# A fused Nystrom attention and expert layer on one core: overlapping landmark transposes and another hand-written order of 1147 operations

## Chip, core and metric

The kernel runs on one core of one Trainium2 chip. The metric is the device time of one execution in microseconds (us). Five engines work in parallel, each through its own instructions in order: PE (matmul, with weight loads shown as PEld), DVE, ACT, POOL (GpSimd) and SP, which here only issues DMAs. POOL issues DMAs too.

## What is computed

Attention over 8 batches of 8 heads, 576 rows and 64 columns, with 32 landmarks per head, and behind it a mixture of 8 experts over the 4608 tokens that come out. Cut to what matters:

```
q_lm = q.reshape(B, H, 32, 18, D).mean(axis=3)        # landmarks: means of 18 rows
k_lm = k.reshape(B, H, 32, 18, D).mean(axis=3)
A, Bm, C = softmax(q k_lm^T), softmax(q_lm k_lm^T), softmax(q_lm k^T)    # each scaled
Z = Bm^T / (norms); six times Z = 2 Z - Z Bm Z
attn = A Z C v
x = attn as (tokens, 512)
e = argmax(x w_gate); gate = max(softmax(x w_gate)); eom = sigmoid(x w_output_gate)
out = gate * eom * (relu(x w1[e]) w2[e])               # per token, by its expert
```

## The kernel before

The work is a list of 1147 operations, built batch by batch in program order, each with a kind, the engines that may do it, and what it reads and writes. `Plan.op` records them; `Plan.emit` then emits them in the order of the string `ORDER`, whose words are an operation's number and a letter for the engine that does it (p PE, v DVE, a ACT, g POOL, s SP). An operation's tile is taken from its tag's free list when its first operation is emitted, and given back behind its last. So `ORDER` sets each engine's queue, the choice among engines, and which buffer a value gets. There is no scheduler at run time: an engine waits for the instruction at its head.

**Attention** (`attend`), for each batch and each half (four heads):
- Three loads on SP (`bring`; L379 to L383): k, q, v. Each tag has three buffers, and a load waits until the fourth load before it (in program order) has landed.
- Batches 0 to 2 are *wide* ones (turned batches): PE transposes k and q in 128x128 blocks (L414), four or two to an operation, and ACT or DVE copies each result out (L302, L308). The landmark sums, one for k and one for q, are done by DVE (a reduction over the 18 rows, L433, and a copy, L434) or by POOL (`tree`: a chain of adds, L326 to L335) into the tile s9; two transpositions on PE (L442) and a scaling copy on ACT or DVE (L314, L316) make the landmarks lm.
- Batches 3 to 7 are *narrow*: DVE transposes k and q (L448) and the sums are taken of the result (L458 on DVE, `tree` on POOL).
- Scores on PE (L475), maximum on DVE (L492), exponential on ACT (L499), transposition of the result EC on PE (L511) and product with v (pv, L522). The other softmax, At, goes over DVE (L536, L539, L545, L547, L553), POOL (L541, L549), and ACT (L543); a cast (L304 on POOL, L302 on ACT) makes Ab_all of it.

**Iteration and routing** (`solve`, `finish`), by groups of batches 0, 1, 2, 3, (4, 5), (6, 7): scores of the landmarks with each other (L578), their softmax, column sums (L606), seven rounds of small matmuls on PE (L627), each evacuated by ACT or DVE (L314, L316), a block form BD (L640), its product with Y (L658), logits (L670, L689), a chain of small DVE instructions (L714 to L759) with one *count* on PE (L732) in it, which ends with the batch's main expert.

**Experts** (`ffn`): POOL reads the expert's number and asks for w1 (L263) and w2 (L266), in halves for batches 0, 1, 6 and 7, if it is another than that of two batches before. PE multiplies w1 by the small matrix Mb (*mix*, L818), ACT or DVE copies the result U out as bf16, then come 16 *up* operations (L832), each with a relu on ACT or DVE (L300, L306), and five row tiles of the *down* product (L850; L853 for the last 64 rows), each in two halves of four w2 blocks (fc 0 to 3, and 4 to 7), scaled on ACT or DVE (L862, L864) and stored by SP (L875, L881). Weights have two buffers, batches alternating. Tokens of other experts than the main one would be done by a loop at the end, when there are any.

PSUM holds two tiles S of two banks (scores, EC, mix) and four tiles M of one bank (all else).

The code that the change touches, besides `ORDER`:

Of the kernel before, what the change touches and what calls it, by code (L numbers as in the profile page):

```python
# [28 lines left out]
ADD = mybir.AluOpType.add  # L29
# [86 lines left out]
ORDER = """0s 14v 1s 15g 35s 51v 36s 52g 5p 2s 9p 10a 11p 3p 4a 48p 49v 6a 167s 168s 44p 12v 13a 37s  # L116
7p 16p 8v 50v 38s 45v 17a 18p 40p 19v 202s 41a 26v 27v 178p 42p 53p 20a 21p 203s 169s 182g 54v 46p
172p 22a 181v 179a 47a 72p 43a 332s 55p 173a 73v 74a 28g 56v 170p 171a 75v 57a 333s 176p 23p 204s 183p 63v
64v 216g 180a 174p 177a 29a 217v 211p 175a 58p 205p 65g 212a 184a 207p 367s 77p 59a 185p 206a 30v 24v 25a 66a
76v 78v 31v 32g 335p 67v 218p 79p 336a 186v 80v 208a 209p 60p 219v 187a 33v 81p 210a 68v 188p 346g 82a 83p  # L120
193v 194v 195g 213p 368s 189a 215a 61v 334s 69g 84a 343p 214a 62a 495s 347v 220p 341p 342v 345a 85p 86a 87p 88a
70v 381g 337p 228v 229v 230g 89p 496s 376p 520s 90a 338a 344a 91p 92v 221v 237p 372p 377a 196a 370p 191v 39g 238v
373a 197v 222a 190p 93p 239a 198v 231a 369s 94v 199g 96p 97v 98p 192a 223p 240v 382g 371a 232v 99v 378p 339p 224a
348p 100a 638s 380a 101v 226v 200v 349a 103p 233v 234g 379a 225p 521s 340a 350p 104v 497s 227a 351v 242p 383p 352a 241v
243v 107g 384v 235v 374p 244p 245v 105a 375a 353p 354a 498v 95g 71g 34g 402p 246p 247a 248p 249a 500g 358v 385p 403v
499v 355p 404a 663s 359v 360g 250p 251a 252p 522s 393v 111p 253a 639s 386v 112a 108g 501g 405v 119p 394v 102a 407p 387a
254p 255a 388p 406v 395g 523v 361a 389a 256p 408v 127p 257v 120a 362v 258p 128a 356v 357v 390p 259a 261p 524v 409p 640s
262a 263p 410a 391v 110g 396a 411p 260a 264v 397v 392a 502p 265a 412a 413p 266v 363v 526g 503v 713s 115p 116a 268p 414v
415p 269v 504a 664s 505a 113p 267v 364g 416a 270a 129p 117p 114a 109g 417p 642v 130a 418a 365v 525g 121p 506p 122a 118a
# [37 lines left out]
def kernel(  # L167
# [106 lines left out]
    with tc.manual_schedule():  # L274
# [46 lines left out]
        def tree(src, to, c):  # L321
# [672 lines left out]
```

## Time and profile before

| | us |
|---|---|
| median of 3 runs (lowest, highest) | 242.16 (241.96, 243.62) |
| the profiled execution, its own time | 239.26 |
| its span, first to last instruction | 237.6 |
| PE busy in it | 207.1 |
| DVE busy | 178.9 |
| POOL busy | 144.4 |
| ACT busy | 132.2 |

All stretches, durations and waits below are of the profiled execution, and count from the start of its span. A busy PE is one with a matmul in its pipeline; matmuls overlap, and the ends are modelled. In a group's row stand the count, the busy time, the mean duration in ns, and then the idle time before its instructions with what ended it. In a list of waits stand the total, the number of waits and the longest. In a timeline the first column is the start, the second the duration.

### The profile page before, as it was taken

How to read it: one execution, taken by the hardware profiler on the slowest of the kernel's cores; microseconds unless marked ns; L12 is line 12 of the kernel's file. 1: busy time of each engine (PE TensorE's matmuls, PEld its weight loads, DVE VectorE, ACT ScalarE, POOL GpSimd, SP SyncE). 2: the span in 40 equal slices, each digit the busy share in tenths (PEclk: the TensorE clock that was granted, in tenths of full speed). 3: DMA queues.
4: the chain of work that ended last, by engine and by line, in shares of the span. 5: the costliest groups of instructions: out<-in, count | busy, mean ns of one | idle time of the engine just before them, and what ended most of it. 6: DMA issues, size and time to landing. Idle time of an engine off the chain costs nothing.

```text
span 237.6 us, 9458 instructions
## 1 busy us (share of the span) xinstructions
PE 207.1 (87%) x3905; PEld 138.2 (58%) x3921; DVE 178.9 (75%) x433; ACT 132.2 (56%) x339; POOL 144.4 (61%) x226
## 2 busy tenths in 40 slices
PE   1878987687679999999999999999999999999960
PEld 1756756454555567657655776676567555655630
DVE  4887998898688899898789997899778642515330
ACT  2357848547365568456766645654776174526320
POOL 5879498789986799698826998835261064200000
PEclk9999999999999999999999999999999999999995
DMA  6999888899999799997966435407677369999445
GB/s 247 348 302 305 295 269 292 269 175 302 220 272 225 135 193 288 278 307 170 295 210 188 146 102 168 149 3 129 133 135 124 116 135 210 237 228 198 136 122 179
DMA packets 34847, 48.92 MB, mean 206 GB/s; under 512 B 7664, under 2 KB 26096, under 8 KB 34800
## 3 DMA queue, kind: packets, MB, share of 16 engines
q1 hardware_dynamic: 24640, 37.79, 51.0%
q0 software_dynamic: 10160, 10.49, 28.9%
q8 instruction: 32, 0.52, 0.9%
q14 instruction: 15, 0.12, 0.2%
HBM read 61.90 MB, written 9.44 MB: 300 GB/s over the span
## 4 chain that ended last, share of the span: by engine, by line
PE 63%; DMA 14%; DVE 8%; issue 5%; ACT 4%; POOL 2%; SPq 1%; POOLq 0%; DVEq 0%; ACTq 0%
PE M L850 21%; PE M L832 12%; PE S L475 9%; DMA nq<-in_q_dram 7%; DMA w<-in_moe_w_dram 7%; PE M L627 5%; PE M L853 3%; PE S L511 3%; PE M L522 3%; PE M L689 2%; PE S L818 1%; PE M L414 1%; DVE s L433 1%; PE M L658 1%; ACT U L302 1%
## 5 line engine op out<-in xcount | busy, mean ns | idle before, releaser
L850 PE MATMUL M<-w,hT 128*128 128x512 bf16 x241 | 58.2, 380 | 1.2 <-issue 0.7
L300 ACT ACTIVATE hT<-M 128x288 bf16<-128x288 f32 x96 | 34.9, 411 | 16.8 <-PE M L832 15.8
L832 PE MATMUL M<-Ab_all,U 128*128 128x288 bf16 x256 | 40.4, 287 | 1.9 <-ACT U L302 1.3
L850 PEld LDWEIGHTS <-hT 128*128 128x128 bf16 x256 | 28.0, 114 | 23.2 <-issue 2.2
L329 POOL TENSOR_TENSOR folds<-folds 128x256 f32<-128x256 f32 (+1 forms) x48 | 28.4, 592 | 3.8
L832 PEld LDWEIGHTS <-U 128*128 128x128 bf16 x256 | 22.2, 97 | 14.4 <-issue 3.8
L475 PE MATMUL S<-Tk,lm 32*32 32x288 f32 (+1 forms) x416 | 27.7, 407 | 1.1 <-ACT Tk L302 0.6
L862 ACT ACTIVATE y<-M,co 128x512 f32<-128x512 f32 (+1 forms) x23 | 15.3, 668 | 22.5 <-PE M L850 21.3
L475 PE MATMUL S<-Tq,lm 32*32 32x288 f32 (+1 forms) x416 | 27.2, 403 | 0.2 <-issue 0.2
L263 POOL DMA_DIRECT2D w<-in_moe_w_dram x24 | 11.8, 493 | 23.8 <-PE M L832 11.5
L549 POOL TENSOR_TENSOR At<-At,st 128x576 f32<-128x576 f32 x16 | 18.5, 1159 | 8.8 <-DVE st L547 5.4
L541 POOL TENSOR_TENSOR At<-At,st 128x576 f32<-128x576 f32 x16 | 18.5, 1159 | 7.9 <-DVE st L539 7.7
L864 DVE TENSOR_SCALAR y<-M,co 128x512 f32<-128x512 f32 (+1 forms) x17 | 11.1, 652 | 16.3 <-ACT y L862 6.0
L306 DVE TENSOR_SCALAR hT<-M 128x288 bf16<-128x288 f32 x32 | 13.9, 450 | 12.2 <-PE M L832 11.7
L627 PE MATMUL M<-X 32*32 32x64 f32 (+1 forms) x768 | 17.9, 214 | 5.6 <-issue 3.4
L627 PEld LDWEIGHTS M<-X 32*32 32x32 f32 x768 | 12.5, 104 | 13.1 <-issue 6.2
L475 PEld LDWEIGHTS S<-Tk,lm 32*32 32x32 f32 (+1 forms) x416 | 15.4, 104 | 4.6 <-ACT Tk L302 1.0
L314 ACT ACTIVATE X<-M 128x128 f32<-128x128 f32 (+1 forms) x30 | 9.3, 310 | 14.4 <-PE M L627 14.4
L475 PEld LDWEIGHTS S<-Tq,lm 32*32 32x32 f32 (+1 forms) x416 | 14.0, 105 | 2.3 <-issue 0.8
L499 ACT ACTIVATE EC<-S,st 128x576 f32<-128x576 f32 x16 | 11.9, 744 | 5.3 <-DVE st L316 2.5
L492 DVE TENSOR_REDUCE st<-S 128x1 f32<-128x576 f32 x16 | 11.9, 746 | 3.4 <-PE S L475 3.4
L414 PE MATMUL M<-I,nk 128*128 128x128 f32 x54 | 9.9, 308 | 5.2 <-DMA nk<-in_k_dram 4.9
(144 smaller groups left out, 437.8 us busy)
## 6 DMA issues: line engine op xcount, KB each, us to landing
nk<-in_k_dram SPq DMA_DIRECT2D x16, 576.0 KB, 5.2
nq<-in_q_dram SPq DMA_DIRECT2D x16, 576.0 KB, 5.3
nv<-in_v_dram SPq DMA_DIRECT2D x16, 512.0 KB, 5.8
w<-in_moe_w_dram POOLq DMA_DIRECT2D x16, 512.0 KB, 9.8
out_dram<-y SPq DMA_DIRECT2D x32, 256.0 KB, 4.4
w<-in_moe_w_dram POOLq DMA_DIRECT2D x16, 256.0 KB, 8.2
w<-in_moe_w_dram POOLq DMA_DIRECT2D x4, 1024.0 KB
nv<-in_v_dram SPq DMA_DIRECT2D x16, 64.0 KB, 5.8
```

Source lines behind the costliest of these rows:

```text
L300: nc.scalar.activation(out=dst(), in_=src(), func=RELU)
L306: nc.vector.tensor_scalar(out=dst(), in0=src(), scalar1=0.0, scalar2=None, op0=MAX)
L329: add(s[:, :, :n // 2], s[:, :, :n // 2], s[:, :, n // 2:n // 2 * 2], op=ADD)
L414: nc.tensor.transpose(pT.t[:, c * 128:(c + 1) * 128], in_=ns[y].t[:, 2 * t:2 * t + 2].rearrange("p t d -> p (t d)"), identity=I128)
L475: nc.tensor.matmul(p.t[o * m:(o + 1) * m, n, :U2], lhsT=l_of(lm, wide, 0 if x == "k" else 1, h, n if wide else j), rhs=t_of(Ts[x], wide, n ...
L492: P.op("cmaxw" if wide else "cmax", ("DVE",), lambda e, pC=pC, st=st, wide=wide: nc.vector.tensor_reduce(st.t[:, 1:2] if wide else st.t[:, ...
L541: P.op("asub", ("POOL",), lambda e, At=At, st=st: nc.gpsimd.tensor_tensor(At.t, At.t, bc(st.t[:, 8:8 + g], g, m), op=SUB), r=[st["ax"]], w ...
L549: P.op("amul", ("POOL",), lambda e, At=At, st=st: nc.gpsimd.tensor_tensor(At.t, At.t, bc(st.t[:, 32:32 + g], g, m), op=MUL), r=[st["as"]], ...
L627: nc.tensor.matmul(pN.t[r_, u * W + lo:(u + 1) * W], lhsT=cur.t[r_, u, :m] if it else nx.t[r_, u], rhs=cur.t[r_, u, lo:], start=(it == 0 a ...
L832: nc.tensor.matmul(ph.t[:, :NH], lhsT=Uw.t[:, hf, fc * 128:(fc + 1) * 128], rhs=Ab_all[:, b, hf, n * NH:(n + 1) * NH], start=(hf == 0), st ...
L850: nc.tensor.matmul(py.t, lhsT=of_tile(hTs[fc].t, i), rhs=w2.t[:, fc, :], **f)
L862: nc.scalar.activation(out=y.t[:, :n], in_=py.t[:, :n], func=COPY, scale=com.t[:, i:i + 1])
```

## The change

Two things change. In s9 the sums of a wide half stand as q, k, q (three columns blocks of 64) in place of q, q and k, k. PE's first transposition takes columns 0 to 127 (q, k), the second 64 to 191 (k, q), so each lands with q and k on either half of the partitions; the reader takes the other tile for the upper half (`x ^ j`). k's sum is written once: on DVE the copy behind it is dropped, on POOL the last add writes 64 columns. q's sum is still written twice. The second thing is the whole string `ORDER`: another order, and another engine for some operations. Line numbers move by one or two (L414 is L415 in the change, L442 L444, L475 L477, L818 L820, and so on).

```
-ORDER = """0s 14v 1s 15g 35s 51v 36s 52g 5p 2s 9p 10a 11p 3p 4a 48p 49v 6a 167s 168s 44p 12v 13a 37s
...
+ORDER = """1s 15g 9p 10v 7p 8a 0s 5p 6a 3p 4a 14v 11p 13v 12a 16p 17a 36s 52g 35s 51v 40p 41v 42p
...
-    t_s9 = tag("s9", 2, [128, 2, 2, D])
+    t_s9 = tag("s9", 2, [128, 3, D])
...
             if j == 1:
-                add(to, bt(s[:, 0, 0], 2, c), bt(s[:, 0, g // 2 - 1], 2, c), op=ADD)
+                n = to.shape[1]
+                add(to, bt(s[:, 0, 0], n, c), bt(s[:, 0, g // 2 - 1], n, c), op=ADD)
...
             if wide:
-                return lm.t[j * D:(j + 1) * D, x, h * m:(h + 1) * m]
+                return lm.t[j * D:(j + 1) * D, x ^ j, h * m:(h + 1) * m]
...
                             if e == "DVE":
-                                nc.vector.tensor_reduce(s9.t[:, i, 0], n.t.rearrange("p t d -> p d t"), axis=X, op=ADD)
-                                nc.vector.tensor_copy(s9.t[:, i, 1], s9.t[:, i, 0])
+                                nc.vector.tensor_reduce(s9.t[:, i], n.t.rearrange("p t d -> p d t"), axis=X, op=ADD)
+                                if i == 0:
+                                    nc.vector.tensor_copy(s9.t[:, 2], s9.t[:, 0])
                             else:
-                                tree(n.t.rearrange("p t (j c) -> p j t c", j=1), s9.t[:, i], D)
-                        P.op("sum", ("POOL", "DVE"), sums, r=[ns[x][0]], w=[s9[i]], b=b)
+                                tree(n.t.rearrange("p t (j c) -> p j t c", j=1), s9.t[:, 0:3:2] if i == 0 else s9.t[:, 1:2], D)
+                        P.op("sum" + x, ("POOL", "DVE"), sums, r=[ns[x][0]], w=[s9[i]], b=b)
...
-                            nc.tensor.transpose(pD.t[:, i * 128:(i + 1) * 128], in_=s9.t[:, i].rearrange("p a d -> p (a d)"), identity=I128)
+                            nc.tensor.transpose(pD.t[:, i * 128:(i + 1) * 128], in_=s9.t[:, i:i + 2].rearrange("p a d -> p (a d)"), identity=I128)
```

Of the operations that may run on either of two engines, these change: of the 12 wide sums DVE had 5 and has 4 (all of k), POOL 7 and 8; of the 20 narrow sums DVE had 3 and has 1, POOL 17 and 19; of the 16 evacuations of U DVE had 4 and has 1, ACT 12 and 15; of the 24 evacuations of four turned blocks DVE had 3 and has 7, ACT 21 and 17; of the 6 scalings of landmarks DVE had 3 and has none; of the 16 casts to Ab_all POOL had 10 and has 5. The rest are single small ones.

Three places of the order follow. The first is PE's queue where batch 0 gets its landmark scores (L578, in the change L580). nk0 to nk2 and nq0 to nq2 are loaded k and q, s90 and s91 the tiles s9 of the two halves, lm0 and lm1 the landmarks, EC0 an exponential. Before:

```order
L414 MATMUL M3_168<-I128_61,nk1_85 128x128 x4
L442 MATMUL M2_167<-I128_61,s91_95 128x128 x2
L511 MATMUL S1_164<-I128_61,EC0_100 128x128 x5
L414 MATMUL M0_165<-I128_61,nq1_82 128x128 x4
L414 MATMUL M2_167<-I128_61,nk2_86 128x128 x4
L578 MATMUL M0_165<-lm0_96 32x32 x4
L578 MATMUL M0_165<-lm1_97 32x32 x4
L475 MATMUL S0_163<-Tk1_93,lm1_97 32x288 x8
```

In the change:

```order
L444 MATMUL M2_167<-I128_61,s91_95 128x128 x2
L415 MATMUL M3_168<-I128_61,nq2_83 128x128 x4
L580 MATMUL M0_165<-lm0_96 32x32 x4
L580 MATMUL M0_165<-lm1_97 32x32 x4
L415 MATMUL M1_166<-I128_61,nk2_86 128x128 x4
L415 MATMUL M3_168<-I128_61,nq1_82 128x128 x4
L513 MATMUL S1_164<-I128_61,EC0_100 128x128 x5
L415 MATMUL M2_167<-I128_61,nk0_84 128x128 x4
L415 MATMUL M1_166<-I128_61,nk2_86 128x128 x4
L608 MATMUL M3_168<-Bn0_129,own_67 128x64
L477 MATMUL S0_163<-Tk1_93,lm1_97 32x288 x8
```

The landmark scores stand ahead of the transposition of EC instead of behind it, and the column sums of the same batch (L608) follow five rows later, ahead of the second half's scores; before, they stand 13 rows after the landmark scores.

The second place is PE's queue from the end of batch 0's first mix on (w100 is w1, U0 the evacuated product). Before:

```order
L818 LDWEIGHTS Mb_all_138
L818 MATMUL S1_164<-w100_159,Mb_all_138 32x512
L832 LDWEIGHTS U0_139
L832 MATMUL M0_165<-Ab_all_137,U0_139 128x288
...
L606 MATMUL M1_166<-Bn0_129,own_67 128x64
L627 MATMUL M3_168<-X1_109 32x64 x8
L511 MATMUL S1_164<-I128_61,EC1_101 128x128 x5
```

In the change:

```order
L820 LDWEIGHTS Mb_all_138
L820 MATMUL S0_163<-w100_159,Mb_all_138 32x512
L444 MATMUL M2_167<-I128_61,s90_94 128x128 x2
L415 MATMUL M0_165<-I128_61,nq2_83 128x128 x4
L629 MATMUL M1_166<-X0_108 32x64 x8
L477 MATMUL S1_164<-Tk0_92,lm0_96 32x288 x8
L477 MATMUL S0_163<-Tq0_90,lm0_96 32x288 x8
L444 MATMUL M2_167<-I128_61,s91_95 128x128 x2
L415 MATMUL M3_168<-I128_61,nk2_86 128x128
L415 MATMUL M3_168<-I128_61,nq2_83 128x128
L524 MATMUL M0_165<-nv0_87,ECT0_102 32x64 x20
L580 MATMUL M2_167<-lm0_96 32x32 x4
```

The first up (L832) follows the mix at once before, and batch 1's column sums and iteration come behind it; in the change turns, scores and landmark scores of batch 2 stand between them.

The third place is POOL's queue at the second half of batch 1's w2 (w210; L266). folds is the scratch tile of POOL's sums, st and At belong to the second softmax, w100 is batch 2's w1. Before:

```order
L335 TENSOR_TENSOR lm0_96<-folds_79 128x64
L266 ISA
L266 DMA w210_162<-in_moe_w2_dram 128x4x512
L304 CAST Ab_all_137<-AT_all_105 128x576
L266 ISA
L266 DMA w210_162<-in_moe_w2_dram 128x4x512
L549 TENSOR_TENSOR At0_103<-At0_103,st0_113 128x576
```

In the change:

```order
L336 TENSOR_TENSOR lm1_97<-folds_79 128x64
L790 TENSOR_LOAD main_i_75
L795 TENSOR_LOAD new_i_76
L263 ISA
L263 DMA w100_159<-in_moe_w1_dram 64x4x1024
L263 ISA
L263 DMA w100_159<-in_moe_w1_dram 64x4x1024
L543 TENSOR_TENSOR At1_104<-At1_104,st5_118 128x576
L551 TENSOR_TENSOR At0_103<-At0_103,st2_115 128x576
L266 ISA
L266 DMA w210_162<-in_moe_w2_dram 128x4x512
```

Before, one cast stands between the two halves' requests. In the change a sum, batch 2's request for w1 and two instructions on At stand there, and further sums of batch 4 and instructions on At stand ahead of the first half's.

More of the change, by code (lines that the diff above doesn't have):

```diff
@@ L121 @@
[L121 to L125, printed above, removed]
@@ new lines @@
+216v 86v 66a 67v 68v 69g 175v 209p 210v 29a 30v 31v 32g 368s 347g 58p 59a 213p 214a 215v 87p 88a 89p 90a
+185p 186v 60p 62a 369s 207p 495s 208a 70v 339p 187a 91p 92v 93p 94a 95a 96p 97a 33v 98p 34a 218p 219a 237p
+71a 340a 211p 496s 193v 194v 212a 99v 100a 101v 103p 102a 105a 335p 336a 381g 238v 239a 104v 107g 108g 106a 220p 240v
+241v 191v 370p 371a 372p 373a 221v 222a 228v 229v 230g 343p 337p 338a 242p 243v 341p 342a 346v 223p 344a 195g 226v 499v
+244p 224a 225p 334s 520s 382g 110g 245a 345a 231a 232v 196a 233v 234g 188p 189a 521s 197v 198v 199g 111p 112a 348p 349a
```

87 lines of the change are left out of this document (43 added, 44 removed).

## The prediction

> **What bounds the kernel now.** I read the page first, then busy time by stretch (columns: stretch, its length, then busy time and count of PE, PEld, DVE, ACT, POOL, then PE's clock, DMA share and GB/s), then what PE waited for.
>
> ```profile
> span 237.6 us, 9458 instructions
> PE 207.1 (87%) x3905; PEld 138.2 (58%) x3921; DVE 178.9 (75%) x433; ACT 132.2 (56%) x339; POOL 144.4 (61%) x226
> ```
> ```profile
> 0.00:4.80 4.80, 0.00 (x0) 0.01 (x1) 1.72 (x10) 1.30 (x2) 3.34 (x21) 1.00 0.57 213
> 4.80:70.00 65.20, 51.30 (x1126) 37.60 (x1127) 57.36 (x138) 38.10 (x105) 54.37 (x75) 1.00 0.97 279
> 70.00:230.00 160.00, 155.79 (x2782) 100.54 (x2795) 119.83 (x287) 92.17 (x233) 86.64 (x131) 1.00 0.76 178
> 230.00:237.60 7.60, 0.00 (x0) 0.00 (x0) 0.00 (x0) 0.67 (x1) 0.00 (x0) 0.66 0.51 159
> ```
> ```profile
> PE M L414 <- DMA nk<-in_k_dram: 4.9, 1, 4.9
> PE M L627 <- issue: 3.4, 3, 2.0
> PE M L414 <- DMA nq<-in_q_dram: 1.9, 4, 0.7
> PE M L832 <- ACT U L302: 1.3, 2, 1.1
> ```
> The 30.5 us in which PE does nothing lie in four places: 4.8 before the first load lands, 13.9 between 4.8 and 70, 4.2 in the 160 us to 230, and 7.6 at the end, where the last output leaves. From 70 on the time is PE's own work, and an order cannot shorten work. So what another order can win lies before 70, and what it can lose lies anywhere. Before 70 the waits of PE are many and small (the list after the first load holds nothing over 3.4), because DVE is busy 57.4 of 65.2 us there and POOL 54.4: PE waits for results that stand in the queues of two engines that are nearly as full as itself.
>
> **The landmark sums.** The group of DVE's sums, all instances of the copy behind them, and the longest of these copies with the POOL instruction beside it:
>
> ```profile
> L433 DVE TENSOR_REDUCE s<-nk 128x64 f32<-128x1152 f32 x3 | 6.4, 2148 | 1.8 <-DMA nk<-in_k_dram 1.8
> L433 DVE TENSOR_REDUCE s<-nq 128x64 f32<-128x1152 f32 x2 | 4.4, 2206 | 1.2 <-DMA nq<-in_q_dram 1.2
> L434 DVE COPY s<-s x5: 194/196/940, 6.9 to 33.1; 128x64 f32<-128x64 f32 x5
> ```
> ```profile
> 33.10 0.94 DVE L434 COPY s<-s 128x64 f32<-128x64 f32 x1
> ```
> ```profile
> 32.83 1.16 POOL L549 TENSOR_TENSOR At<-At,st 128x576 f32<-128x576 f32 x1
> ```
> Now five of twelve sums run on DVE, each with its copy; in the change four do, all of k, and k needs no copy. The five copies are 2.3 us of DVE (the group's five times 457 ns mean), of which three take 0.2 and two four times that. The long one above began at 33.10 and ended at 34.04, with the POOL instruction that ended at 33.99. The Trainium skill (SBUF — State Buffer, Who interferes with whom) says that a copy of DVE may take a port pair shared with GpSimd and that the later of two then fully blocks; the trace agrees, by that 0.94. PE's part is the same two transpositions. On POOL q's last add still writes 128 columns and k's writes 64. So this part is worth at most 2.3 us of DVE, counted below with the rest of DVE's queue.
>
> **The order, measured in work.** To compare orders I cut PE's timeline into its 386 operations and took for each kind the median distance from its start to the next start: 0.59 us for a turn of four blocks, 1.13 for wide scores, 2.12 for narrow ones, 0.36 for a round of one batch's iteration, 0.70 for pv, 0.59 for a transposition of EC, 0.25 for an up, 0.86 for half a down. Over all 386 this is 203.9 us in either order, since the operations are the same, and PE changes its tiling 161 times now and 162 times in the change. A place in the new order is then dated by the moment at which PE has as much work behind it now:
>
> ```profile
> 32.98 0.43 PE L627 MATMUL M<-X 32*32 32x64 f32 x16
> 42.23 0.38 PE L442 MATMUL M<-I,s 128*128 128x128 f32 x2
> 43.70 0.36 PE L732 MATMUL M<-rt,ones 128*128 128x8 f32 x2 [1.08 <-ACT Tq L302]
> 54.39 0.41 PE L818 MATMUL S<-w,Mb_all 64*32 64x512 bf16 x7 [0.29 <-DMA w<-in_moe_w_dram]
> 55.93 0.42 PE L832 MATMUL M<-Ab_all,U 128*128 128x288 bf16 x2 [1.13 <-ACT U L302]
> 70.52 0.43 PE L627 MATMUL M<-X 32*32 32x64 f32 x16
> 103.14 0.63 PE L818 MATMUL S<-w,Mb_all 64*32 64x512 bf16 x16
> ```
> *Batch 0's chain.* Its count (L732) has 34.6 us of PE work ahead of it now and comes at 43.70; in the change 26.0, which PE has behind it now at 32.98. I take 36: three us later than the work alone, since fewer other operations cover the seven rounds. Its first mix (L818, seven of eight matmuls at 54.39) moves from 42.8 to 33.7 of work (now reached at 42.2), its first up (L832) only from 43.1 to 40.6. So today's wait for the evacuated U (1.13 before the first up) is covered by 6.9 us of other work, and is gone. But the weights take their time behind the count:
>
> ```profile
> 46.49 1.47 POOL L263 DMA_DIRECT2D w<-in_moe_w_dram  x2 [0.74 <-DVE st L492]
> ```
> ```profile
> DMA to landing us min/median/max: 7.9/8.2/8.5
> ```
> 2.8 us from count to issue and 8.2 to landing make 11.0: the mix can run at 47.0. PE comes to it 7.7 us of work after the count, at 43.7 plus what it waits for on the way. Up to 3.3 us of wait arise at the mix, behind which the turns and scores of batch 2 queue, and 2 at most go at the first up: no gain by itself.
>
> *Up to 74.* The last gate of the first stage are the narrow scores of batch 3's second half (now at 56.5 of work, in the change at 53.0, reached now at 70.5). They need the last of four sums on POOL, and DVE's maximum of the first half.
>
> ```profile
> 4.80:65.50 60.70, 48.34 (x1074) 35.63 (x1074) 52.97 (x123) 34.95 (x96) 50.12 (x70) 1.00 0.97 280
> 4.80:70.60 65.80, 51.90 (x1133) 38.03 (x1137) 57.96 (x139) 38.65 (x107) 54.86 (x76) 1.00 0.97 280
> ```
> DVE has 53.0 us ahead of that maximum (65.5). In the change 14.1 us of what stands there moves behind it or to other engines (three sums with copies, three scalings of landmarks, small ones), 10.3 comes in (six evacuations of four blocks, two sums of k), and copies of sums that stay save 0.9: 4.7 less. If DVE idles as now, everything behind comes 4.7 earlier: the upper bound of the gain. POOL has one sum more ahead of the fourth narrow sum's end (+3.6), three casts and a subtraction fewer (-2.9): +0.7. If POOL idles as now, the fourth sum ends at 71.3 (now at 70.6) and the scores start with 53.0 of work done, where 54.1 is done now: a loss of 1.1, the lower bound. Neither engine says which; I take the middle, **1.8 gained**. The SP queue carries the same loads in another order, those of v later; the first use of each lies several operations behind, and PE's longest wait for one after the first is under 1.
>
> *Batch 1's second weights.* The second half of w2 of batch 1 is issued on POOL behind batch 4's sums instead of ahead of them.
>
> ```profile
> 4.80:46.50 41.70, 34.85 (x650) 25.73 (x650) 37.06 (x82) 24.82 (x67) 32.84 (x45) 1.00 0.94 300
> 4.80:84.80 80.00, 65.87 (x1370) 46.80 (x1372) 70.30 (x162) 47.08 (x126) 64.89 (x92) 1.00 0.97 265
> ```
> ```profile
> 50.23 1.42 POOL L326 TENSOR_TENSOR folds<-Tk 128x576 f32<-128x576 f32 x1 [0.76 <-DVE Tk L448]
> 53.76 1.16 POOL L541 TENSOR_TENSOR At<-At,st 128x576 f32<-128x576 f32 x1
> 84.82 0.76 POOL L266 DMA_DIRECT2D w<-in_moe_w_dram  x1
> ```
> ```profile
> DMA to landing us min/median/max: 6.3/8.4/10.5
> ```
> POOL has 64.9 us behind it at this issue. In the change four sums more (3.53 each, from 50.23 to 53.76), four of L541 and L549 more (1.16), three casts (0.67), four small copies (1.0) fewer, and batch 2's request (0.5): +16.2. That gives 4.8 + 81.1 = 85.9 plus POOL's idle time: 8.9 if it idles as up to the first request (41.7 less 32.8), 10.9 as up to 70.6, 15.1 as up to 84.8. Issue at 94.8 to 101.0, landing 6.3 to 10.5 later, at 101.1 to 111.5. PE comes to the first half down that reads it (fc 4 to 7) after 85.4 of work, at 103.1 now, so at 101.3 with the 1.8 gained; the narrow scores of batch 5 queue behind it. Today the half lands at 95.3 at the latest (84.82 and 10.5). A wait of 0 to 10.2 follows. POOL has more work at hand than now, so it should idle less: I take 9.9, midway between the two smaller, and the transfer that has less beside it, 6.3: landing at 102.1, **0.8 lost**.
>
> The Trainium skill (DMA: Bandwidth & Descriptors, Anatomy of one DMA) gives for a transfer issued by GpSimd 2.0 us plus the bytes at 436 GB/s: for the 1.05 MB read here an estimate of 4.4. The shortest in this trace is 6.3, and the traces decide. By the rule the half would land at 100.2, ahead of PE, nothing be lost there, and the sum be 240.4.
>
> *After that.* Batch 2's request is done in no time, as its expert is the one whose weights lie there:
>
> ```profile
> 97.33 0.06 POOL L263 DMA_DIRECT2D w<-in_moe_w_dram  x1 [1.12 <-DMA w<-in_moe_w_dram]
> ```
> PE's work ahead of the counts of batches 5 and 7 and of the mixes of batches 3 to 7 differs by under 4 us, and mostly to the earlier side. At the end the same half down, one scaling and one store come last:
>
> ```profile
> 229.98 0.69 ACT L862 ACTIVATE y<-M,co 128x512 f32<-128x512 f32 x1 [0.99 <-PE M L850]
> ```
> Nothing there.
>
> **Sum.** -1.8 + 0.8 = -1.0 on the profiled execution's 239.26 (span 237.6 and 1.7 around it), 238.3. That execution is 2.9 below the median of the runs, 242.16, so the forecast is **241.2**: no change that can be told, as 1% (2.4 us) is about what a measurement of this kernel tells from none.
>
> **Rivals.** *The first stage wins its full bound.* DVE keeps as busy as now, all comes 4.7 earlier, and the half of w2 lands in time: 242.2 - 4.7 = 237.5. For it: DVE is busy 53.0 of 60.7 us there, with few gaps. Against: batch 0's iteration, drawn together, leaves DVE less to do between its rounds, and POOL's queue is no shorter. Chance 0.33. *The half of w2 comes late (slower).* One place, POOL's queue ahead of L266 of batch 1: if POOL idles 15.1 as now, the issue is at 101.0, the landing 8.4 later at 109.4, PE waits 8.1, less 1.8: 248.5. It decides from an issue after 98. For it: the 16.2 us are counted, and the idle time of POOL is waits for DVE's results, in order. Against: DVE delivers earlier. Chance 0.27. *The change does not do what it says.* The copies go but the gates stay where they are, since what PE waits for before 70 is latency: then 242.2, within the middle case. The middle case, within 1%, has 0.40.
>
> **How the numbers follow.** The middle case has its own range, 239.8 to 244.6. To leave out no more than 2 in 10 the range reaches to a gain of 5.7, the first rival and one us of luck, and to a loss of 5.3, most of the second rival: 236.5 to 247.5. Faster 0.33, same 0.40, slower 0.27.
>
> **What would show it.** Right: the count of batch 0 at 35 to 37 and its first mix at 46 to 48 with a wait on the weights before it; DVE less busy over the span by some 11 us, and POOL more by some 6; a wait of PE at L850 on w or on POOL's transfer near 102; PE's work after that without holes. The stretch 4.8 to 70 should still show PE idle for 11 to 14 us. Wrong: PE idle there under 10 (the first rival), or a hole of 4 us and more at L850 near 103 (the second), or holes after 110, which no term here has.

## The result, and the profile after

The change makes the kernel slower: 253.62 us (median of 4, 250.39 to 257.85) against 242.89 (median of 4), 1.0454 times the time before, with a 95% interval of 1.0361 to 1.0547. The prediction was 241.2 with a range of 236.5 to 247.5. Some executions are disturbed and run longer: the one profiled with this result (257.85) was, so the rows below are of a second profiled execution of the same kernel (251.82), those profiled for e10, e14 and e15 were too, and ratios leave disturbed executions out while medians have them all, so that a group of runs with too many of them has a median here and no ratio.

First two rows of the page of before that the prediction did not show, PE's busy tenths and the clock that PE was granted, in 40 slices of the span:

```profile
PE   1878987687679999999999999999999999999960
PEclk9999999999999999999999999999999999999995
```

The same of the changed kernel, with its span and busy times:

```profile
span 250.1 us, 9440 instructions
...
PE 215.5 (86%) x3903; PEld 139.6 (56%) x3921; DVE 171.6 (69%) x424; ACT 136.3 (55%) x347; POOL 150.7 (60%) x234
...
PE   2969749887896997998899799999999899999990
...
PEclk9999995997799799999999999999999999999999
```

Two things are new. PE has gaps up to the 24th slice (150 us) where it had them up to the 12th, and its clock falls to half in several places, which it did nowhere in the profiled execution of before until the last output. PE's busy time grew by 8.4 us with the same matmuls, and I put that down to those at half clock. DVE lost 7.3 us of work and POOL gained 6.3; the prediction had some 11 and some 6.

To find the place I used the prediction's own scale: PE's timeline cut into its 386 operations, each at its median cost in before, so that a place is named by the work that PE has behind it. Lag is how much later PE gets there than in before (negative: earlier). The last three columns belong to experiments told below.

| PE work done, us | before, at | changed, lag | clock held (e4) | chain covered (e16) | three repairs (e18) |
|---|---|---|---|---|---|
| 8 | 14.8 | -1.2 | -0.9 | -1.3 | -1.4 |
| 16 | 23.4 | -0.3 | -0.9 | -1.4 | -1.0 |
| 24 | 30.6 | 3.1 | 3.7 | 0.7 | 0.9 |
| 32 | 40.9 | 4.6 | 3.9 | 2.2 | 2.4 |
| 40 | 50.3 | 3.7 | 3.4 | 1.4 | 2.0 |
| 56 | 73.3 | 4.6 | 3.9 | 4.9 | 4.0 |
| 64 | 81.5 | 8.6 | 4.1 | 8.9 | 4.2 |
| 72 | 89.6 | 10.8 | 9.1 | 11.1 | 6.4 |
| 88 | 105.5 | 12.8 | 10.2 | 12.2 | 7.6 |
| 200 | 226.0 | 14.2 | 13.9 | 16.4 | 10.1 |

Each column is one execution. That of before is 2.9 below its median, so a lag is larger than the difference of the medians; that of e4 is the slowest of its five (251.75 with a median of 249.31).

So the change does win a microsecond in the first 15 us, loses four to five between 23 and 45 us, some six between 78 and 100, and three to four up to 146. Behind that the lag stays, until the last 10 us give 1.7 back (9.9 us against 11.6 in before, which ends at half clock). The same stretches of work as busy time by stretch (columns as in the prediction), before:

```profile
23.40:40.90 17.50, 15.18 (x370) 10.72 (x368) 16.62 (x37) 12.61 (x35) 13.47 (x18) 1.00 0.88 282
40.90:73.30 32.40, 24.24 (x627) 17.54 (x620) 27.27 (x85) 18.52 (x54) 28.25 (x42) 1.00 1.02 248
73.30:89.60 16.30, 15.93 (x307) 9.94 (x308) 15.45 (x41) 8.76 (x22) 12.84 (x19) 1.00 0.96 179
89.60:131.80 42.20, 41.23 (x836) 27.11 (x845) 37.44 (x88) 28.26 (x73) 31.57 (x49) 1.00 0.82 244
```

and in the changed kernel:

```profile
23.10:45.40 22.30, 17.14 (x301) 12.44 (x302) 15.98 (x45) 12.64 (x36) 17.16 (x24) 0.85 0.87 263
45.40:77.90 32.50, 27.57 (x692) 17.54 (x691) 28.03 (x65) 19.99 (x57) 26.37 (x36) 0.89 0.79 196
77.90:100.40 22.50, 17.98 (x291) 10.19 (x282) 13.84 (x40) 11.03 (x28) 18.10 (x26) 0.92 0.86 205
100.40:146.10 45.70, 42.00 (x941) 28.67 (x946) 39.88 (x88) 30.87 (x83) 33.24 (x52) 1.00 0.74 215
```

In the first of these PE is idle for 5.2 us where it was idle for 2.3, and in the third for 4.5 where it was 0.4; the rest of the difference is PE at 0.85 and 0.92 of its clock. Two waits make up most of the third place's 4.5, one ahead of an up at 81.3 and one ahead of batch 1's count at 97.0:

```profile
PE M L834 <- issue: 2.2, 1, 2.2
PE M L734 <- DVE rt L728: 1.4, 1, 1.4
```

For the first the profile shows no cause. A stop of 2.1 to 2.7 us stands at this place of PE's instructions in six profiles with the new order (the two of the changed kernel, e3, e6, e10, e16) and in none of e4, e5, e7, e11, e17 and e18; before has one of 2.0 at another place (63.1). No run here tests what it is, so it is a rival to waits and clock for part of the third place.

**The first place.** What PE waits for up to there in before, and in the changed kernel (in us, times, longest):

```profile
PE M L670 <- POOL wgs L392: 0.5, 1, 0.5
PE S L475 <- ACT Tk L302: 0.5, 1, 0.5
PE M L627 <- ACT X L314: 0.4, 1, 0.4
```
```profile
PE M L734 <- DVE M L590: 1.9, 1, 1.9
PE M L629 <- ACT X L314: 1.0, 2, 0.6
PE M L415 <- DMA nq<-in_q_dram: 1.0, 1, 1.0
PE M L660 <- DVE BD L642: 0.7, 1, 0.7
```

and how they stand in PE's timeline (start, duration, and in brackets the idle time before):

```profile
30.48 0.63 PE L415 MATMUL M<-I,nq 128*128 128x128 f32 x4 [0.96 <-DMA nq<-in_q_dram]
...
32.07 0.44 PE L660 MATMUL M<-BD,Y 128*64 128x128 f32 x4 [0.71 <-DVE BD L642]
32.93 0.27 PE L672 MATMUL M<-wgs,ZT 128*32 128x32 f32 x8 [0.41 <-ACT ZT L314]
33.49 0.77 PE L691 MATMUL M<-AT_all,G_all 128*32 128x128 f32 x32 [0.29 <-ACT G_all L302]
...
37.81 0.57 PE L734 MATMUL M<-rt,ones 128*128 128x8 f32 x2 [1.86 <-DVE M L590]
```

This is batch 0's chain, from its last round to its count: each step needs another engine's result of the step before, and the new order has put nearly nothing between them. The count comes at 37.8 in place of 43.7, as an order that hurries batch 0 should have it; but what stood beside the chain in before (batch 1's turns, the transposition of its EC, a product with v, scores) now comes after it, and its results, buffers and loads with it.

### The profile page after: what moved, and what is told of

Read it like the earlier page. It is cut to its first block, busy times and chain, and to the rows that moved or that the text cites. A ratio compares the mean times of both kernels' runs of the same rounds, so it can differ in the third digit from the quotient of the medians.

```text
span 256.1 us, 9440 instructions
## 1 busy us (share of the span) xinstructions
PE 220.8 (86%) x3903; PEld 142.3 (56%) x3921; DVE 171.5 (67%) x424; ACT 136.0 (53%) x347; POOL 150.5 (59%) x234
## 5 line engine op out<-in xcount | busy, mean ns | idle before, releaser
L852 PE MATMUL M<-w,hT 128*128 128x512 bf16 x239 | 61.7, 391 | 1.3 <-issue 0.6
L834 PE MATMUL M<-Ab_all,U 128*128 128x288 bf16 x256 | 43.4, 292 | 3.8 <-issue 2.2
L300 ACT ACTIVATE hT<-M 128x288 bf16<-128x288 f32 x96 | 35.6, 413 | 17.3 <-PE M L834 16.5
L852 PEld LDWEIGHTS <-hT 128*128 128x128 bf16 x256 | 28.1, 116 | 24.6 <-issue 4.8
L329 POOL TENSOR_TENSOR folds<-folds 128x256 f32<-128x256 f32 (+1 forms) x54 | 31.9, 591 | 4.2
L477 PE MATMUL S<-Tk,lm 32*32 32x288 f32 (+1 forms) x416 | 28.5, 439 | 0.5 <-ACT lm L314 0.5
L477 PE MATMUL S<-Tq,lm 32*32 32x288 f32 (+1 forms) x416 | 27.8, 437 | 0.0
L551 POOL TENSOR_TENSOR At<-At,st 128x576 f32<-128x576 f32 x16 | 18.4, 1159 | 13.6 <-DVE st L549 11.0
L263 POOL DMA_DIRECT2D w<-in_moe_w_dram x24 | 11.8, 495 | 23.5 <-DVE need_i L898 11.3
L543 POOL TENSOR_TENSOR At<-At,st 128x576 f32<-128x576 f32 x16 | 18.4, 1157 | 11.3 <-DVE st L541 7.7
L306 DVE TENSOR_SCALAR hT<-M 128x288 bf16<-128x288 f32 x32 | 13.8, 451 | 13.9 <-PE M L834 13.6
L629 PEld LDWEIGHTS M<-X 32*32 32x32 f32 x768 | 13.1, 109 | 12.9 <-issue 6.0
L302 ACT CAST U<-S 128x1024 bf16<-128x1024 f32 x15 | 15.2, 1013 | 6.6 <-PE S L820 6.5
L477 PEld LDWEIGHTS S<-Tk,lm 32*32 32x32 f32 (+1 forms) x416 | 14.4, 110 | 6.3 <-issue 2.2
L415 PE MATMUL M<-I,nq 128*128 128x128 f32 x54 | 10.5, 316 | 6.8 <-DMA nq<-in_q_dram 6.8
L547 DVE TENSOR_REDUCE st<-At 128x18 f32<-128x576 f32 x16 | 11.7, 729 | 5.8 <-ACT At L545 5.7
L326 POOL TENSOR_TENSOR folds<-Tq 128x576 f32<-128x576 f32 x10 | 14.1, 1410 | 2.3 <-DVE Tq L450 2.1
```

The lines of the kernel that those rows point to most:

```text
L300: nc.scalar.activation(out=dst(), in_=src(), func=RELU)
L302: nc.scalar.copy(dst(), src())
L306: nc.vector.tensor_scalar(out=dst(), in0=src(), scalar1=0.0, scalar2=None, op0=MAX)
L326: add(s, src[:, :, :g // 2], src[:, :, g // 2:], op=ADD)
L329: add(s[:, :, :n // 2], s[:, :, :n // 2], s[:, :, n // 2:n // 2 * 2], op=ADD)
L477: nc.tensor.matmul(p.t[o * m:(o + 1) * m, n, :U2], lhsT=l_of(lm, wide, 0 if x == "k" else 1, h, n if wide else j), rhs=t_of(Ts[x], wide, n ...
```

## The experiments

The time is the median, the ratio is to runs of the kernel before on the same chip, half clock is the time for which PE was granted half its clock, worked out for each execution as twice the span times what its mean clock lacks, as a mean over the executions. Over 33 executions of the kernel before that ran beside the experiments it was 10.7.

| kernel | us | ratio (interval) | half clock, us |
|---|---|---|---|
| e1 the change again | 252.12 | 1.0443 (1.0336 to 1.0550) | 20.6 |
| e2 old order, new s9 | 241.90 | 1.0004 (0.9957 to 1.0052) | 11.3 |
| e3 new order, old s9 | 253.24 | 1.0449 (1.0362 to 1.0536) | 24.7 |
| e4 change, clock held | 249.31 | 1.0276 (1.0191 to 1.0361) | 4.0 |
| e5 change, product early | 251.58 | 1.0411 (1.0350 to 1.0473) | 20.8 |
| e6 change, v loads later | 255.07 | 1.0545 (1.0474 to 1.0616) | 24.6 |
| e7 both moves, clock held | 251.31 | | 4.6 |
| e8 old order, new s9, clock held | 240.62 | 0.9857 (0.9787 to 0.9927) | 5.0 |
| e9 change up to 54 us, then before | 247.32 | 1.0199 (1.0120 to 1.0278) | 16.4 |
| e10 change up to 104 us, then before | 254.63 | 1.0434 (1.0344 to 1.0523) | 24.6 |
| e11 before up to 58 us, then change | 253.38 | 1.0450 (1.0377 to 1.0523) | 18.6 |
| e12 before up to 96 us, then change | 246.15 | | 11.3 |
| e13 kernel before, clock held | 242.67 | 0.9998 (0.9933 to 1.0063) | 6.9 |
| e14 old order with a hole | 247.22 | | 13.6 |
| e15 the same, hole filled | 248.05 | | 10.2 |
| e16 change, chain covered | 254.42 | | 24.1 |
| e17 change, covered, clock held | 249.44 | | 7.4 |
| e18 change, covered, product early, clock held | 248.38 | 1.0223 (1.0156 to 1.0290) | 2.7 |

**Which part of the change?** e1 is the changed kernel itself. e2 and e3 exchange the string alone:

```
e2, in the changed kernel     -ORDER = """1s 15g 9p 10v 7p 8a ...   +ORDER = """0s 14v 1s 15g 35s 51v ...
e3, in the kernel before      -ORDER = """0s 14v 1s 15g 35s 51v ...   +ORDER = """1s 15g 9p 10v 7p 8a ...
```

e1 was to give: 

> The changed kernel, unaltered, beside the others of this group. Theory C (clock): in its profiled execution PE was granted half its clock for 34 us in four stretches that begin behind windows of 3.41 us in which PE was busy for under 1.9; each microsecond at half clock costs about 0.5. Expected: 250 to 255, and again at least three stretches at half clock ahead of the last 10 us, each a multiple of 3.41 long. Theory W (waits): the time goes into PE's own waits, the clock is a side effect: 250 to 255 too; stretches at half clock may fall anywhere. A profile of the same kernel with fewer microseconds at half clock is shorter by half of them by C, and no shorter by W.

e2: 

> The landmark change alone: s9 as q, k, q with the overlapping transpositions, and the order of before. Both theories: 241 to 243, as five copies of 2.3 us in all leave DVE's queue, and PE's work is the same; PE at full clock up to the end. Rival L (layout): the landmark change itself costs, by reading s9 with overlap or by what DVE does earlier: 246 or more.

e3: 

> The new order alone, with s9 as before (q, q and k, k, four copies on DVE and q's and k's sums written twice). Both theories C and W: 250 to 256, the loss is the order's. Rival L: 245 or less.

e2 measures 1.0004 and e3 1.0449. The landmark change by itself is worth no more than half a per cent either way; the loss is the order's.

**Is it the clock?** In the changed kernel the clock falls in steps of 3.41 us, each behind a stretch of that length in which PE was little busy. Busy time by such stretches (the second number is PE, the third from the end the clock):

```profile
34.10:37.50 3.40, 1.57 (x42) 0.97 (x28) 1.61 (x8) 2.06 (x5) 3.01 (x6) 1.00 1.02 320
37.50:40.90 3.40, 3.09 (x38) 1.81 (x38) 2.05 (x15) 1.77 (x8) 0.36 (x2) 0.50 0.53 205
40.90:44.30 3.40, 3.40 (x29) 2.94 (x15) 2.58 (x6) 1.52 (x3) 3.26 (x5) 0.50 0.61 93
44.30:47.80 3.50, 3.07 (x73) 2.61 (x72) 2.96 (x7) 3.50 (x10) 3.42 (x4) 1.00 1.06 161
...
78.50:81.90 3.40, 1.22 (x12) 0.60 (x9) 1.74 (x3) 1.12 (x4) 3.32 (x5) 0.99 1.12 173
81.90:85.30 3.40, 3.18 (x13) 1.39 (x11) 2.38 (x5) 1.70 (x4) 3.09 (x5) 0.50 1.05 228
85.30:88.70 3.40, 3.40 (x17) 1.77 (x16) 1.14 (x2) 1.41 (x3) 3.02 (x6) 1.00 0.21 64
```

e4 keeps PE busy where it waits: ahead of 16 operations it transposes the identity into columns that nobody reads.

```
+HOLD = {339: 12, 93: 5, 96: 5, 98: 3, 218: 3, 103: 14, 220: 4, 370: 6, 225: 4, 350: 4, 353: 6, 407: 10, ...}
...
+            self.keep(o, HOLD.get(o.seq, 0))
             o.fn(o.eng)
...
+        def keep(o, n):
+            for _ in range(n):
+                x = [v for v in o.vals if v.tag.name in ("S", "M")][-1]
+                t = x.t[:, 1] if x.tag.name == "S" else x.t
+                nc.tensor.transpose(t[:, 384:512], in_=I128, identity=I128)
```

> The changed kernel with 98 idle transpositions of the identity on PE, put ahead of 16 operations at which PE waits between 28 and 70 us (12 ahead of the turn that waits for a load, 14 ahead of the count of batch 0, 10 ahead of batch 2's column sums, 3 to 6 ahead of the others); each waits only for its PSUM buffer, writes columns that are not read, and takes about 0.11 us. Nothing else is moved. Theory C: with PE busy in these windows the clock stays full there; of the 27 us at half clock between 30 and 72 at most 7 are left, and the time falls by 6 to 13, to 241 to 247. Theory W: the waits are where they were, 10 us of work are added: 252 to 260.

(The list adds up to 93, not 98.) Half clock falls from 20.6 to 4.0 us, and the time by 2.8, to 249.31: less than theory C asked, and not the rise of theory W. At 64 of work the lag is 4.1 in place of 8.6, but at 72 it is 9.1 again, and this execution ends as late as that of e1. So the clock is a part, and something else waits behind it. The 2.8 us for 16.6 us less at half clock, 0.17 for each, contain the cost of the 93 idle transpositions, and the stop at 81.3 is not in e4's profile either.

Its price was then to be measured where the wait is the same. e14 and e15 are the order of before with the new s9, idle work at nine operations, and one load moved, so that PE has a hole at 31; e15 fills it.

```
 e14, e15, order:   ... 332s ... -333s ... 368s +333s ...
 e15 alone:         +HOLD = {..., 343: 32}
```

> The order of before with the new s9 and the 43 idle transpositions, and one load put later on SP: batch 2's first q goes out behind three other loads. It should land at 33 to 35 in place of 27.2, and PE, which needs it at 30.1, stands for 3 to 5 us. Theory C: the window is busy for under 1.5 of 3.41, half clock follows for at least one window, and the time is 3 to 5 (the wait) and 2 to 6 (the clock) above the same kernel without the moved load: 246 to 251. Rival: the clock does not fall or costs nothing: 243 to 245.

> The same with 32 idle transpositions (3.4 us) ahead of the turn that waits for the moved load. The wait is the same; PE is busy in it. Theory C: the clock stays full, and the time lies 2 to 6 below the kernel with the hole left empty: 243 to 246. Rival: the same time as with the empty hole, within 1.

e14, the hole in the second row:

```profile
28.70:32.10 3.40, 2.53 (x76) 1.78 (x64) 2.80 (x7) 2.95 (x9) 3.09 (x5) 1.00 0.77 248
32.10:35.50 3.40, 1.64 (x35) 0.88 (x36) 1.66 (x1) 0.27 (x1) 3.40 (x4) 1.00 1.08 339
35.50:38.90 3.40, 3.00 (x45) 1.93 (x46) 3.23 (x6) 0.55 (x2) 2.11 (x5) 0.50 0.74 293
38.90:42.30 3.40, 3.40 (x58) 2.77 (x59) 1.99 (x5) 2.10 (x5) 1.51 (x2) 0.50 0.54 175
```

e15, the same place:

```profile
32.20:35.60 3.40, 3.40 (x44) 3.09 (x50) 1.51 (x1) 0.41 (x2) 3.40 (x4) 1.00 1.08 351
35.60:39.00 3.40, 3.00 (x81) 1.82 (x65) 3.26 (x5) 0.55 (x2) 2.35 (x5) 1.00 0.79 298
```

In these executions the hole is followed by 6.8 us at half clock, and filling it keeps the clock. At 40 of work e14 lags before by 5.9 and e15 by 4.4: 1.5 us for 6.8 at half clock, 0.2 for each, in one pair of executions and one place (at 64 the two lags are 8.3 and 4.1, at 140 they are 6.6 and 8.2). The times do not price it: four executions each, from 242.70 to 247.88 and from 241.92 to 249.84, and in the fastest of each PE was at half clock for only 5.8 and 4.8 us. That theory C is wrong on the size rests on e4: 2.8 us where it asked for 6 to 13. Half a clock is not half the speed here; PE's waiting for other engines anyway is the likely reason. The executions say something similar: over the 33 of the kernel before the span grows by 0.14 us for each microsecond at half clock, over 7 of the changed kernel by 0.25; with the longest executions kept in (56, without one of 1078.69, and 8) it is 0.24 and 0.32. The changed kernel has 22.2 against 10.7 in the first set, 11.5 more: at 0.14 to 0.32 that is an estimate of 1.6 to 3.7 of its ten microseconds. It is no more than an estimate, as the two going together does not show which makes which.

e8 and e13 hold the clock in the order of before, with the new and the old s9, by 43 idle transpositions (not 40):

> The order of before with the new s9, and 40 idle transpositions ahead of 9 operations at which PE waits between 17 and 70 us. The profiled execution of before ran at full clock, that of the same order with the new s9 had 10.2 us at half clock (two stretches between 56 and 73) and was 2.0 longer. Theory C: no stretch at half clock is left ahead of the end, 239 to 241, faster than before. Rival: the idle work costs what the clock gives, 241 to 243.

> The kernel before, unaltered (its order, its s9), with the same 43 idle transpositions ahead of 9 operations as in the kernel that has the order of before with the new s9. Theory C: the gain there came from the clock and not from s9: 239 to 241 here too. Rival: it came from the copies that left DVE: 242 here.

e8 came out at 0.9857 (four executions, from 237.67 to 243.40), e13 at 0.9998 (ten). Half clock fell in both, to 5.0 and 6.9. As s9 alone is worth 1.0004, the two ought to agree, and I do not take e8 for a faster kernel: by e13 the idle work costs what the clock gives.

**Is it the loads?** In the changed kernel PE stands 0.96 us for batch 2's q, and DVE's transposition of a k of batch 4 starts at 87.64, when that load has just landed (behind a wait of 2.3 us that is put down to ACT). SP goes through its requests in order, and the load of batch 3's v waits for the product of batch 2 with v (L524), which the new order puts at 73 us (51.7 in before). Behind it stands batch 4's k, which lands 6.1 us after its request. SP's timeline in the changed kernel:

```profile
74.00 0.38 SPq L380 DMA_DIRECT2D nv<-in_v_dram  x1
...
81.39 6.53 SPq L384 DMA_DIRECT2D nk<-in_k_dram  x2
```

e5 moves that product (operation 355) 22 operations earlier on PE (not 17), with what belongs to it; e6 puts two v loads behind the loads that PE needs first; e7 does both and holds the clock.

```
 e5:  ... 407p +355p ... 386v +356v 387a +357a ... -356v ... -355p ... -357a ...
 e6:  ... 203s ... -204s ... -169s ... 333s 332s +204s +169s ...
```

> The changed kernel, with one product moved: batch 2's first product with v (L524) stands behind batch 2's column sums on PE, 17 operations earlier, and the reciprocal and the evacuation that belong to it earlier on DVE and ACT. In the change this product comes at 72 to 76 us, and until then SP holds the load of batch 3's v, with the load of batch 4's k behind it, which lands at 87 to 90. Theory S (SP's queue): the load of v goes out at 60 to 66, batch 4's k lands by 76, DVE no longer idles over 2 us ahead of its transposition, and the time falls by 2 to 5, to 247 to 250. Theory C (the clock alone): PE is not limited by that load; 251 to 254, with the same stretches at half clock.

> The changed kernel with the two loads of batch 1's v put behind the loads of batch 2's q and k on SP. In the change batch 2's q lands at 29.8, beside these two, and PE's turn waits 1.7 for it at 28. Theory S: q lands at 26 to 28, the wait falls under 0.6, the window of 3.41 around 28 is busy for over 2.3, and fewer microseconds lie at half clock between 30 and 45; 248 to 251. Theory R (the chain of batch 0 behind that turn, from its last round to its count, has nothing beside it): the wait moves into the steps up to the count, which stays at 38 to 39, and the clock falls all the same; 251 to 254.

> Both moves together, and the idle transpositions ahead of 16 operations that keep PE busy. Theories S and C together: clock full up to the end, 242 to 246. Theory R: with neither loads nor clock in the way, PE still waits for results of DVE, ACT and POOL in many small pieces that the order of before covered; 246 to 250.

SP in e5 (the same two loads):

```profile
63.64 0.43 SPq L390 DMA_DIRECT2D nv<-in_v_dram  x1
...
71.19 4.68 SPq L394 DMA_DIRECT2D nk<-in_k_dram  x2
```

The loads go out ten us earlier, and DVE makes its transposition at 81.15, but the ratio, 1.0411, cannot be told from e1's 1.0443. In e6 batch 2's turn no longer waits, but another turn of the same line, of batch 1's q at 24.9, does: its load went out at 20.8 in place of 19.8. PE's two longest waits there:

```profile
PE M L744 <- DVE M L600: 1.9, 1, 1.9
PE M L425 <- DMA nq<-in_q_dram: 1.1, 1, 1.1
```

The count (L744 here) stands at 38.9 with the same 1.9 ahead of it: theory R's case in the mechanism, though the time, 255.07, lies above both ranges. e7 (251.31, from 246.61 to 255.20) lies above both of its ranges and is not shown to beat e4. One load taken out of the way does not bring the time back.

**Where along the order?** e9 to e12 join the two orders: the first operations of one, then what is left in the order of the other.

> The order of the change for its first 246 operations (all that starts up to about 55 us), then the remaining operations in the order of before; s9 as in the change. Theory P (two places): some 4 us are lost between 23 and 40 us, where batch 0's iteration has nothing beside it and a turn waits for its load, and some 6 more between 80 and 110 us by what the order does there. 245 to 248: the first loss alone. Theory Q (one cause): whatever is lost behind 55 us follows from batch 1's and 2's steps put back in the first stretch; 249 to 253. If neither: 241 to 243, the first stretch costs nothing by itself.

> The order of the change for its first 465 operations (up to about 104 us), then the remaining operations in the order of before. Theories P and Q: the loss is made by then, 249 to 253. If 245 to 248: part of it comes behind 104 us.

> The order of before for its first 280 operations (up to about 58 us), then the remaining operations in the order of the change. Theory P: the loss of the second place alone, 246 to 250. Theory Q: 241 to 244.

> The order of before for its first 500 operations (up to about 97 us), then the remaining operations in the order of the change. Theories P and Q: nothing of note is lost, 241 to 244. If over 246: the rest of the order costs by itself.

Only e9 lies in a range that was named for it (theory P's); e11 and e12 lie above what either theory allowed. e10 (1.0434) is as slow as the change: all is lost by 104 us. e9 (1.0199) has lost 4.8 at 32 of work, gets 2.9 of that back by 48, and then stands 4.1 at one up for a relu on DVE, a wait that neither parent has; e11 stands 5.2 for w1 at its join, e12 2.0 where the profile shows no cause. So these joins bring waits of their own. That of e10 does not show: the lag in its profile is 16.0 at 80 of work and 15.9 at 140. That e9 and e11 are both slow shows that neither part of the change's order is good with the rest of the other; how the ten microseconds divide they do not tell.

**Covering the chain.** e16 puts three of the operations that stood beside batch 0's chain in before back there (a turn, 211; the transposition of EC, 188; its product with v, 190; each with its evacuation). e17 adds idle work, e18 also the product of e5.

```
 e16:  ... 208a +211p +212a ... 91p +188p +189a 92v ... 96p +190p 97a 33v +191v 98p 34a +192v ...
```

> The changed kernel with three PE operations of batch 1 moved into the bare stretch of batch 0's chain: a turn of the second half's q (from 36 us to ahead of the turn that waits for a load), the transposition of the first half's EC (from 48 us to behind the last round) and its product with v (from 53 us to behind the first of the two small products), each with its evacuation. In the order of before they stand in that stretch too. 1.9 us of PE work then lie where PE waits 4.4 us between 28 and 39. Theory P (bare chain): by 40 us of PE's work the lag behind the kernel before falls by 1.5 to 2.5, and the time to 249 to 251. Rival: what is covered here is lost again further on, where other engines' results set the pace: 251.5 to 253.5.

> The same, with 83 idle transpositions on PE at the 16 operations of the first such kernel (fewer ahead of the covered steps). Theory P and the clock together: 246 to 248.5, below both the covered kernel and the one with idle work alone (249.3). Rival: 249 to 251, as the idle work alone.

> All three repairs in the changed kernel: the three operations of batch 1 beside batch 0's chain, batch 2's first product with v early (so that SP is free for batch 4's k), and the 83 idle transpositions. With the clock held and PE earlier than in the kernel with the early product alone, DVE stood 2.95 us for batch 4's k at 83 us, and PE 1.7 at 87 to 89 for a scaling of y behind it. Theory T (several independent holes, each hidden by the others): that wait of PE disappears, and the time is 244 to 247. Rival: another engine's queue sets the pace between 85 and 100 us; 248 to 251, with new waits of PE of 2 us and more there.

e16 does what was expected in its place: at 32 and 40 of work the lag falls from 4.6 to 2.2 and from 3.7 to 1.4. At 56 it is 4.9 again, and the time is no better (254.42, above both ranges). e17 (249.44, four executions from 246.70 to 255.24) does not decide. In e4, with the clock held, the next obstacle can be read from DVE's timeline:

```profile
86.22 1.38 DVE L452 STREAM_TRANSPOSE Tk<-nk 128x1152 f32<-128x1152 f32 x1 [2.95 <-DMA nk<-in_k_dram]
...
89.78 0.74 DVE L868 TENSOR_SCALAR y<-M,co 128x512 f32<-128x512 f32 x1
```

and PE's longest wait behind it:

```profile
PE M L526 <- DVE y L868: 1.7, 1, 1.7
```

It is batch 4's k, the load of e5: DVE stands for it, the scaling of y stands behind it, and PE waits for the PSUM tile that this frees. In e18, with all three repairs, that wait is gone:

```profile
PE M L746 <- DVE rt L740: 1.4, 1, 1.4
PE M L846 <- ACT Ab_all L314: 0.7, 1, 0.7
PE S L525 <- ACT EC L513: 0.5, 1, 0.5
```

The lag at 72 of work is 6.4 in place of 10.8 (9.1 in e4), and the kernel measures 1.0223 (1.0156 to 1.0290): half of the loss is back. But e4's idle work alone gave 1.0276 (1.0191 to 1.0361), so the times do not show that the other two repairs add to it. At 248.38 it lies above theory T's 244 to 247 and inside the rival's 248 to 251; the wait that T named is gone, and the new waits are shorter than the rival's 2 us. No version here is shown to be faster than the kernel before.

## Why the prediction was wrong, point by point

*The landmark sums.* Right: worth nothing that can be measured (e2), the copies are gone from DVE's queue, and the larger part was said to be DVE's queue as a whole.

*Batch 0's chain.* Nearly right: the count was put at 36 and came at 37.8, the first mix at 47.0 and came at 48.1 (without the wait for its weights that was named as a sign), and "no gain by itself" holds. What was missed is what it costs the others: the chain's waits, counted as latency of batch 0, are idle time of PE, and everything behind is late by them.

*Up to 74.* This is the step that failed: the term of 1.8 gained. Its bounds, 4.7 gained to 1.1 lost, rested on DVE and POOL idling as in before. POOL did: its fourth sum ended at 71.5, where 71.3 was worked out. DVE did not. Up to its maximum of the first narrow half:

```profile
4.80:69.90 65.10, 52.18 (x971) 36.27 (x972) 50.63 (x115) 36.20 (x98) 54.15 (x74) 0.90 0.88 253
```

It has less work ahead of it, 50.6 us in place of 53.0, though only half of the 4.7 less that the count of moved work gave, and comes 4.4 later, since it idles for 14.5 where it idled for 7.7. Its waits in this stretch are mostly for PE:

```profile
DVE Tq L308 <- PE M L415: 3.4, 2, 3.1
DVE M L614 <- PE M L608: 3.1, 3, 1.6
DVE BD L642 <- PE M L629: 2.3, 2, 1.7
```

PE waits for DVE and ACT in the chain, DVE for PE in the same chain: with less other work beside it, both idle together. The narrow scores came at 74.9, where the forecast had 68.7 and its worst bound 71.6. They did not come from either gate: POOL's sum ended at 71.5, DVE's maximum at 70.6, and PE reached them without a wait of its own. PE was late. From 4.8 to there it was idle for 13.1 us, and for 13.9 in before up to the same work; what grew is its busy time, 57.1 in place of 51.8, with 13.7 us at half clock. With the clock held (e4) they came at 74.3, so the pace up to there is not the clock's alone. For the same reason the sign "PE idle for 11 to 14 us from 4.8 to 70" came true (12.9) and told nothing. A place dated by the work ahead of it is right only if that work can run when its turn comes; my allowance for "fewer other operations" was three microseconds on one count and none on the queues behind.

*The loads.* "The first use of each lies several operations behind" was wrong twice: batch 2's q kept PE for 0.96, and batch 4's k kept DVE for 2.95 in e4. I compared the order of the loads, not the operations that free their buffers; the product with v is PE's 96th operation in place of its 71st.

*Batch 1's second weights.* The race was there, with both sides late. The request went out at 107.2 (forecast 95.8), PE came at 115.0 (forecast 101.3), and waited 0.7 (forecast 0.8). That the two sizes agree, with both sides over 11 us off, is luck. On POOL:

```profile
107.19 0.81 POOL L266 DMA_DIRECT2D w<-in_moe_w_dram  x1
```

and on PE:

```profile
PE M L852 <- DMA w<-in_moe_w_dram: 0.7, 1, 0.7
```

The rival that ended slower had the right sign by another mechanism.

*After that.* "Nothing there" was the second failed step: from 56 to 112 of work the lag grows from 4.6 to 14.3. I had compared how much PE work stands ahead of counts and mixes, which had changed by under 4 us, and not who is waited for between them. That there would be holes after 110 which no term has was among the signs named: from 110 to 240 PE is idle for 5.9 us, against 3.2 in before from 110 to 226, and the longest hole (1.5, at 143.9) is again one without a cause in the profile.

*The clock.* No term had it; the views in the prediction showed 1.00 in every stretch but the last. By e4 and the estimate above it takes some two to four microseconds of the ten.

What remains open: of the 5.5 us that e18 is still behind, no single wait of PE behind the first load is larger than 1.4, and I have not shown which of them set the end. That the loss is the new order's is shown (e2, e3), and that half of it goes with the clock held and the two waits covered. That the rest is waits is read from the profiles and not shown by a run, and the stop without a cause at 81.3 is not tested.

## What to carry to other kernels

Here, hurrying one chain by taking the other work away from beside it left PE, DVE and ACT waiting for each other; before trusting an order, count what can run in each of the chain's waits, not how much work stands ahead of its end. In a queue, follow each load back to the instruction that frees its buffer. And where several holes lie behind one another, removing one can show little: e5 and e16 gave nothing alone that the times can tell; that they add to e4's idle work is seen in one profile (a lag of 6.4 against 9.1 at 72 of work), not in the times.

## What the runs showed of the hardware

PE's clock was granted at full or half, in steps of 3.41 us on a grid that stays the same through an execution. Over all 20 profiles there are 1267 such windows at full clock ahead of the end. Of those in which PE was busy for under 1.7 us, 24 of 26 were followed by half clock; of those from 1.7 to 2.1, 13 of 32; from 2.1 to 2.3, 1 of 21; above that, none of 1188. Idle transpositions count as work: in e15 they fill the window from 32.2, and the clock stays full behind it. Back to full it went only behind windows with 3.0 us and more of work, and not always then: 28 windows at half clock were followed by another, the busiest with 3.39. The Trainium skill (TensorE: Matmul & The Clock Gate, Part 1: The HAM clock gate (the "warmup" mystery)) gives the same length, 4096 cycles at 1.2 GHz, and the same two clocks; but it lets the clock fall after an idle window, and in its section on HAM oscillation warns of gaps of more than about 3.4 us. Here the measurement differs: half the window busy was not enough, and in the first profile of the change the four falls ahead of the end came with no single gap of PE over 2.2 us. For each microsecond at half clock these kernels lost 0.17 us where it was taken away (e4), and 0.14 to 0.32 by the spread of the executions, not 0.5.
